# A decode kernel (attention and an MLP, mixed by a gate): sixteen rows of w1 loaded whole to a tile of their own, b1 in three loads

## The chip, the cores and the metric

The kernel runs on one core of one Trainium2 chip. The metric is the device time in microseconds of one execution. Each number given for a kernel is the median of several runs.

## The reference

Eight sequences, one new token each. Attention with 16 query heads over 8 key and value heads of 256, on the last 1,024 positions of a cache; an MLP of 448 to 1,792 to 448 on the layer-normed input; a sigmoid gate that mixes both.

```python
def _A_ref(x, k_cache, v_cache, wq, wo):
    B, Sq, D = x.shape
    Hq, Dh = 16, 256
    Hkv, Sk = k_cache.shape[1], k_cache.shape[2]
    W = min(4096, max(256, Sk // 4))
    rep = Hq // Hkv
    q = (x @ wq).reshape(B, Sq, Hq, Dh).transpose(0, 2, 1, 3)
    k = jnp.repeat(k_cache[:, :, Sk - W:, :], rep, axis=1)
    v = jnp.repeat(v_cache[:, :, Sk - W:, :], rep, axis=1)
    scores = jnp.einsum("bhqd,bhkd->bhqk", q, k) * (Dh ** -0.5)
    p = _softmax(scores, axis=-1)
    o = jnp.einsum("bhqk,bhkd->bhqd", p, v)
    return o.transpose(0, 2, 1, 3).reshape(B, Sq, Hq * Dh) @ wo

def _B_ref(x, w1, b1, w2, b2):
    y = _layernorm(x, axis=-1)
    h = _gelu(jnp.einsum("bsd,df->bsf", y, w1) + b1)
    return jnp.einsum("bsf,fd->bsd", h, w2) + b2

x = A_x
g = _sigmoid((x * gate_w).sum(-1, keepdims=True))
a = _A_ref(x, A_k_cache, A_v_cache, A_wq, A_wo)
b = _B_ref(x, B_w1, B_b1, B_w2, B_b2)
return g * a + (1 - g) * b
```

All tensors are bfloat16. The caches hold 4,096 positions, of which the last 1,024 are read: 33.6 MB of keys and as many of values. wq is 448 x 4,096, wo 4,096 x 448, w1 448 x 1,792, w2 1,792 x 448.

## The kernel before

**Loads.** Nearly all bytes pass through a ring of four slots of 32 KB on each of the 128 partitions (`ring`, `slot`). The list `plan` holds the loads in order: wq; five key quarters (a quarter is the keys of four sequences at a quarter of the positions); then values of one sequence and the next key quarter in turn; the remaining values; w1 (with room for w2 behind it, the slot `w12`); the last sequence's values in two halves, and w2; wo in eight cuts that get smaller. `pump()` issues a load on SP's queue when a slot is free, and `done()` frees one when its last reader has been written down. SP waits for the readers of the slot, and for the completion of an older load where a completion counter is used again (loads take turns on eight counters). The small tensors x and gate_w come on ACT's queue at the start. `biases()`, called after the second key quarter, loads b2 to eight partitions, and b1 as four rows to partitions 0, 32, 64 and 96.

**Order of the work.** The order on each engine is that of the program; it is written out by hand. `query()` projects the queries. For each key quarter `transpose_keys` turns the keys (PE with an evacuation by ACT or DVE; part of each quarter by DVE and POOL), `scores` multiplies. After four quarters a softmax (`top`, `expo`, `turn`) follows, then per sequence `scale`, `bring`, `values`, `finish` and `spread`. `moments()` and `gate()` stand near the start; `norm()` stands after the values of sequence 4, `mlp_hidden()` before the values of the last sequence. The end is `wide` and `narrow`, the matmuls with w2 and wo in the order in which the cuts land, and `run_on` puts matmuls without use between them.

**x, turned.** `turned(a, put, copy)` writes the rows of x (a = 0, for the query) or of the normed x (a = 1, for w1) to a tile `xs`, transposes it on DVE to `xt` and copies it to `xw`, from where PE takes its weights. Rows 0 to 383 of wq and w1 lie three to a partition. The last 64 rows (`DM` to `D`) lie as 128 half rows, one on each partition: half h of row r on partition 2r + h. For these x is written twice, once on the even and once on the odd columns, with the other columns zero (lines 248 and 249), and `ends` makes one matmul for each column quarter pair (line 612).

**w1.** In `mlp_hidden` twelve matmuls (line 601) take the three rows of each partition for four column quarters of 448; the four quarters write to rows 0, 32, 64 and 96 of one PSUM bank. Two more (line 612) add the half rows. Then DVE and ACT compute the GELU and DVE the transposed `hs`.

**Tiles.** `consts` are tiles of their own. `work` tiles share a buffer by tag: w0 holds xs, qs and z in turn, w1 xs and za, w2 xt, qt and zb, w3 xt and zt. `prod` (gate) and `early` (end) lie in `consts`. `shift` is a tile that nothing reads; it moves those behind it, the ring among them.

Of the kernel before, what the change touches and what calls it, by code (L numbers as in the profile page):

```python
# [11 lines left out]
BF16 = mybir.dt.bfloat16  # L12
F32 = mybir.dt.float32
# [4 lines left out]
def kernel(  # L18
# [15 lines left out]
    nc = tc.nc  # L34
    P = nc.NUM_PARTITIONS
# [8 lines left out]
    F = B_w1.shape[1]  # L44
# [31 lines left out]
    TAIL = 12  # L76
    SHIFT = 96
    EARLY = 4
    TURNED = {5: 3, 6: 3, 7: 3}
    FAR = -3.0e38  # L80
# [61 lines left out]
    def rows_loader(pieces):  # L142
        def load(t):
            o = 0
            for ap in pieces:
                n = ap.shape[-1]
                nc.sync.dma_start(t[:, o : o + n], ap)
                o += n

        return load  # L150
# [3 lines left out]
    w1_m = B_w1[0:DM, :].rearrange("(p r) f -> p (r f)", r=NR)  # L154
    w1_t = B_w1[DM:D, :].rearrange("r (h n) -> (r h) n", h=2)
    w2_v = B_w2.rearrange("(p c) n -> p (c n)", c=FB)
# [40 lines left out]
    def biases():  # L197
# [3 lines left out]
        parts = B_b1.rearrange("(t d) -> t d", t=QD)  # L201
        for t in range(QD):
            nc.sync.dma_start(b1_r[BL * t : BL * t + 1, :], parts[t : t + 1, :])

# [9 lines left out]
    xw = consts.tile([P, 2, NX, GAP], BF16)  # L214
    xs = [work.tile([BL, NX, P], BF16, tag=f"w{a}", name="xs") for a in range(2)]
    nc.gpsimd.memset(xs[0][:], 0.0)
# [26 lines left out]
    def turned(a, put, copy):  # L243
        dst = xs[a][0:NB]
        put(
            dst[:, 0:NR, :], x_sb[:, 0:DM].rearrange("b (p r) -> b r p", r=NR)
        )
        for h in range(2):
            put(dst[:, NR + h, h::2], x_sb[:, DM:D])
        xt = work.tile([BL, NX, QD, BL], BF16, tag=f"w{2 + a}", name="xt")  # L250
        nc.vector.transpose(
# [3 lines left out]
        for i in range(QD):  # L255
            copy(xw[BL * i : BL * (i + 1), a, :, BL : BL + NB], xt[:, :, i, 0:NB])  # L256

# [20 lines left out]
    def gate():  # L278
        prod = consts.tile([NB, D], F32)
        gl = consts.tile([NB, 1], F32)  # L280
# [314 lines left out]
    def mlp_hidden():  # L595
        nc.vector.memset(hp, 0.0)
        w = slot("w12")
        for r in range(NR):
            for t in range(QD):
# [7 lines left out]
                    skip_group_check=True,  # L607
                )
        for x2 in range(2):
            lhsT, m = ends(1, x2)  # L610
            o = OW1T + x2 * FQ
            nc.tensor.matmul(
                hp[0:m, :],
                lhsT=lhsT,
                rhs=w[:, o : o + FQ],
                start=False,
# [106 lines left out]
    part = [1, 0, 1, 0, 0, 1, 1, 0, 0, 0, 0, 0, 0]  # L723
    early = consts.tile([2 * BL, DO], F32)
    res = consts.tile([2 * BL, DO], BF16)
# [47 lines left out]
```

## Time and profile before

| what | value |
|---|---|
| median of 3 runs | 189.57 us (189.55 to 190.25) |
| profiled execution | 189.50 us, span 187.6 us, 2,781 instructions |
| PE busy | 126.7 us (68%) |
| DVE, ACT, POOL busy | 94.1 (50%), 72.4 (39%), 80.7 us (43%) |
| bytes moved | 77.85 MB, mean 415 GB/s over the span |
| granted TensorE clock | 0.85 mean |

The profile page gives the span in 40 equal slices, one digit for each, in tenths of busy time:

```
PE   0252498998988987489868985883660167537973
DVE  6602247664654665870653281492045972357711
ACT  2003389691955929740770473274034010001000
POOL 8401591672827538003995999199800000000000
DMA  6999999999999999999999999999999999999991
```

A slice is 4.7 us. Rows of groups, chain and timeline name a line of the kernel (L601), an engine (PE matmul, PEld weight load, DVE, ACT, POOL, SPq for SP's queue of loads), and the tiles, output first. In a timeline row the first number is the start, the second the busy time, and what stands in brackets at the end is the idle time of the engine before it and what ended it. In a row of windows each engine has its busy time and, in parentheses, how many instructions; behind them stand the granted clock, the share of busy time of the 16 DMA engines and the GB/s. The rows of DMA queues have the packets, MB and the share of 16 engines' span.

### The profile page before, as it was taken

What the parts mean: (1) busy time and instruction counts of PE and PEld (TensorE: products, weight loads), DVE (VectorE), ACT (ScalarE), POOL (GpSimd) and SP (SyncE); (2) the same over time, 40 slices, a digit from 0 to 9 for tenths busy, and PEclk for the clock granted to TensorE, in tenths of its full rate; (3) what the DMA queues carried; (4) which work ended last, traced back from release to release, by engine and by line L of the source; (5) the groups of instructions that cost most, each with busy time, mean ns of one, the idle gap of its engine ahead of it and who ended that gap; (6) DMA issues with size and microseconds to landing.
All of it is one profiled execution on the core that took longest, in us unless ns stands there. A gap on an engine that the chain in (4) does not pass through costs nothing.

```text
span 187.6 us, 2781 instructions
## 1 busy us (share of the span) xinstructions
PE 126.7 (68%) x1105; PEld 73.3 (39%) x1106; DVE 94.1 (50%) x161; ACT 72.4 (39%) x87; POOL 80.7 (43%) x157
## 2 busy tenths in 40 slices
PE   0252498998988987489868985883660167537973
PEld 0010485675756655353742671563120012212321
DVE  6602247664654665870653281492045972357711
ACT  2003389691955929740770473274034010001000
POOL 8401591672827538003995999199800000000000
PEclk9999579999999999657997999999576555785798
DMA  6999999999999999999999999999999999999991
GB/s 218 438 465 447 447 412 419 430 414 447 437 447 391 424 470 393 437 423 458 454 398 416 447 426 447 402 440 423 433 433 426 433 423 424 430 423 433 414 400 55
DMA packets 5715, 77.85 MB, mean 415 GB/s; under 512 B 556, under 2 KB 1096, under 8 KB 1864
## 3 DMA queue, kind: packets, MB, share of 16 engines
q1 hardware_dynamic: 5656, 77.68, 97.1%
q8 instruction: 8, 0.13, 0.2%
q10 hardware_dynamic: 48, 0.02, 0.1%
q14 instruction: 3, 0.02, 0.0%
HBM read 77.69 MB, written 0.01 MB: 414 GB/s over the span
## 4 chain that ended last, share of the span: by engine, by line
DMA 27%; PE 25%; POOL 20%; ACT 13%; DVE 11%; issue 3%; SPq 1%; POOLq 0%; ACTq 0%
POOL kt L371 20%; PE ktp L392 14%; DMA slot<-in_A_k_cache_dram 10%; DMA slot<-in_A_wo_dram 9%; ACT kt L396 8%; PE S_ps L467 7%; DMA slot<-in_A_v_cache_dram 7%; PE PO L552 3%; DVE kt L398 2%; ACT E L491 2%; ACT other L491 2%; DVE EB L507 1%; DVE B L357 1%; DVE nmx L480 1%; DVE E L505 1%
## 5 line engine op out<-in xcount | busy, mean ns | idle before, releaser
L371 POOL COPY kt<-B 32x128 f32<-32x128 f32 (+1 forms) x128 | 72.3, 565 | 42.9 <-PE S_ps L467 24.9
L392 PE MATMUL ktp<-ident_f,slot 128*128 128x128 f32 x456 | 64.5, 292 | 14.1 <-DMA slot<-in_A_k_cache_dram 5.9
L396 ACT COPY kt<-ktp 128x1024 bf16<-128x1024 bf16 x57 | 56.3, 1015 | 45.7 <-PE ktp L392 45.7
L392 PEld LDWEIGHTS ktp<-ident_f,slot 128*128 128x128 f32 x456 | 52.4, 148 | 27.8 <-ACT kt L396 11.1
L398 DVE COPY kt<-ktp 128x1024 bf16<-128x1024 bf16 x57 | 38.9, 688 | 31.5 <-PE ktp L392 31.0
L467 PE MATMUL S_ps<-kt,qw 128*16 128x512 bf16 x256 | 21.1, 459 | 12.1 <-POOL kt L371 9.3
L552 PE MATMUL PO<-slot,ET 128*16 128x512 bf16 x256 | 23.3, 523 | 4.8 <-DVE rstd L321 2.0
L357 DVE STREAM_TRANSPOSE B<-slot 128x512 f32<-128x512 f32 (+1 forms) x8 | 8.8, 1105 | 14.4 <-DMA slot<-in_A_k_cache_dram 9.9
L467 PEld LDWEIGHTS <-qw 128*16 128x16 bf16 x256 | 6.6, 92 | 23.8 <-issue 13.4
L552 PEld LDWEIGHTS <-ET 128*16 128x16 bf16 x256 | 7.8, 113 | 18.1 <-issue 11.8
L527 PE MATMUL sm<-EZ,perm 128*128 128x128 bf16 x8 | 2.0, 248 | 13.5 <-DVE EZ L514 13.5
L409 PE MATMUL S_ps<-slot,xw 128*8 128x512 bf16 x24 | 2.9, 617 | 10.7 <-DVE xw L256 7.1
L480 DVE TENSOR_REDUCE nmx<-S_ps 128x1 f32<-128x2048 f32 x2 | 4.6, 2292 | 9.8 <-PE S_ps L467 9.8
L567 DVE STREAM_TRANSPOSE T<-PO 128x512 f32<-128x512 f32 x8 | 5.7, 706 | 7.4 <-PE PO L552 7.4
L629 ACT ACTIVATE zb<-za 128x448 f32<-128x448 f32 x1 | 0.6, 576 | 19.1 <-DVE za L628 19.1
L491 ACT ACTIVATE E<-S_ps,nmx 128x1024 f32<-128x1024 f32 x2 | 4.1, 2036 | 9.7 <-DVE nmx L480 9.7
L527 PEld LDWEIGHTS <-perm 128*128 128x128 bf16 x8 | 0.8, 100 | 16.9 <-DVE EZ L514 16.9
L447 POOL COPY qw<-qt 32x64 bf16<-32x64 bf16 x8 | 2.2, 277 | 11.3 <-DVE qt L434 11.0
L535 DVE TENSOR_TENSOR ET<-sm,mask 128x512 bf16<-128x512 f32 x8 | 5.5, 686 | 1.1 <-PE sm L527 1.0
L434 DVE STREAM_TRANSPOSE qt<-qs 128x512 bf16<-128x512 bf16 x2 | 1.3, 690 | 8.8 <-ACT qs L431 8.8
L702 PE MATMUL warm<-slot,ident 128*128 128x512 bf16 (+1 forms) x17 | 5.4, 421 | 0.2 <-issue 0.2
L409 PEld LDWEIGHTS <-xw 128*8 128x8 bf16 x24 | 0.6, 100 | 12.0 <-POOL b_r L239 7.1
(91 smaller groups left out, 68.9 us busy)
## 6 DMA issues: line engine op xcount, KB each, us to landing
slot<-in_A_k_cache_dram SPq DMA_DIRECT2D x8, 4096.0 KB, 30.2
slot<-in_A_v_cache_dram SPq DMA_DIRECT2D x7, 4096.0 KB, 25.1
slot<-in_A_v_cache_dram SPq DMA_DIRECT2D x2, 2048.0 KB
slot<-in_A_wq_dram SPq DMA_DIRECT2D x1, 2048.0 KB
slot<-in_A_wo_dram SPq DMA_DIRECT2D x2, 896.0 KB
slot<-in_B_w_dram SPq DMA_DIRECT2D x1, 1568.0 KB
slot<-in_B_w_dram SPq DMA_DIRECT2D x1, 1344.0 KB, 22.4
slot<-in_A_wo_dram SPq DMA_DIRECT2D x3, 448.0 KB, 20.6
```

What stands on the lines that cost most here:

```text
L357: nc.vector.transpose(B[:].rearrange("p c w x -> p (c w x)"), kn[:, 0 : n * P],)
L371: nc.gpsimd.tensor_copy(words[BL * w : BL * (w + 1), BL * g : BL * (g + 1), 0:n, 0], B[BL * g : BL * (g + 1), :, w].rearrange("p c x -> p ...
L392: nc.tensor.transpose(words[:, c, :, 0], kn[:, o : o + P], ident_f[:])
L396: nc.scalar.copy(dst, src)
L398: nc.vector.tensor_copy(dst, src)
L467: nc.tensor.matmul(S_ps[BL * t : BL * t + HR, k * QN : (k + 1) * QN], lhsT=qf[:, o : o + HR], rhs=KT[0][:, x : x + n, :, j], start=False, ...
L480: nc.vector.reduce_max(nmx[:], S_ps[:], axis=AXIS.X, negate=True)
L491: nc.scalar.activation((E[:, 0:W], other[:])[u].rearrange("p (c k s) -> p k s c", k=KQ, c=NCK), S_ps[:].rearrange("p (k u s c) -> p u k s ...
L535: nc.vector.tensor_tensor(ET[:].rearrange("p c u a r -> p (c u) a r"), sm[:] .rearrange("p k (o r) -> p k o r", o=1) .to_broadcast([P, NCK ...
L552: nc.tensor.matmul(PO[BL * t : BL * t + Hq], lhsT=ET[:, c].rearrange("p u a r -> p (u a r)"), rhs=vn[:, c], start=(c < QD), stop=(c >= NCK ...
L567: nc.vector.transpose(T[:, 0 : NG * n], PO[:].rearrange("p u (e j) -> p u j e", j=J8))
L702: nc.tensor.matmul(warm[:, 0:m], lhsT=ident[:], rhs=slot("v", NB - 1)[:, 0:m], start=True, stop=True,)
```

## The change

Of w1's last 64 rows 48 are loaded as before, as half rows, now to 96 partitions. The last sixteen are loaded whole, to a tile `w1x` of 16 partitions, in one transfer whose source is four times four rows: row 4j + i goes to partition 4i + j. The transfer is issued after b1 on SP's queue. x gets a sixth block for these rows (a = 1 only), which goes by way of `xt` to the tile `x1x`, and `mlp_hidden` gets four matmuls with it, one for each column quarter. b1 is loaded in three transfers (rows 0 and 1, row 2, row 3). `prod` and `early` move to `work` buffers w0 and w1, and `shift` grows from 96 to 120 columns; with it the ring, and all that lies behind, lies 1,024 bytes further than before on each partition. SP issues as many loads as before.

```diff
-    SHIFT = 96
+    SHIFT = 120
     EARLY = 4
+    NE = 4 * QD
...
-                nc.sync.dma_start(t[:, o : o + n], ap)
+                nc.sync.dma_start(t[0 : ap.shape[0], o : o + n], ap)
...
-    w1_t = B_w1[DM:D, :].rearrange("r (h n) -> (r h) n", h=2)
+    w1_t = B_w1[DM : D - NE, :].rearrange("r (h n) -> (r h) n", h=2)
+    w1_e = B_w1[D - NE : D, :].rearrange("(j i) f -> i j f", i=4)
+    NT = w1_t.shape[0]
...
-        for t in range(QD):
-            nc.sync.dma_start(b1_r[BL * t : BL * t + 1, :], parts[t : t + 1, :])
+        for t, n in ((0, 2), (2, 1), (3, 1)):
+            nc.sync.dma_start(b1_r[BL * t : BL * (t + n) : BL, :], parts[t : t + n, :])
+        nc.sync.dma_start(w1x[:], w1_e)
...
-    xs = [work.tile([BL, NX, P], BF16, tag=f"w{a}", name="xs") for a in range(2)]
+    xs = [
+        work.tile([BL, NX + a, P], BF16, tag=f"w{a}", name="xs") for a in range(2)
+    ]
+    w1x = consts.tile([NE, F], BF16)
+    x1x = consts.tile([BL, NB], BF16)
...
+        n = P - a * (P - NT)
         for h in range(2):
-            put(dst[:, NR + h, h::2], x_sb[:, DM:D])
-        xt = work.tile([BL, NX, QD, BL], BF16, tag=f"w{2 + a}", name="xt")
+            put(dst[:, NR + h, h:n:2], x_sb[:, DM : DM + n // 2])
+        if a:
+            put(
+                dst[:, NX, 0:NE].rearrange("b (i j) -> b i j", i=4),
+                x_sb[:, D - NE : D].rearrange("b (j i) -> b i j", i=4),
+            )
+        xt = work.tile([BL, NX + a, QD, BL], BF16, tag=f"w{2 + a}", name="xt")
...
-            copy(xw[BL * i : BL * (i + 1), a, :, BL : BL + NB], xt[:, :, i, 0:NB])
+            copy(xw[BL * i : BL * (i + 1), a, :, BL : BL + NB], xt[:, 0:NX, i, 0:NB])
+        if a:
+            copy(x1x[:], xt[:, NX, 0, 0:NB])
...
-        prod = consts.tile([NB, D], F32)
+        prod = work.tile([NB, D], F32, tag="w0", name="prod")
...
+        for t in range(QD):
+            nc.tensor.matmul(
+                hp[BL * t : BL * t + NB, :],
+                lhsT=x1x[0:NE, :],
+                rhs=w1x[:, t * FQ : (t + 1) * FQ],
+                start=False,
+                stop=False,
+                skip_group_check=True,
+            )
         for x2 in range(2):
             lhsT, m = ends(1, x2)
             o = OW1T + x2 * FQ
             nc.tensor.matmul(
                 hp[0:m, :],
-                lhsT=lhsT,
-                rhs=w[:, o : o + FQ],
+                lhsT=lhsT[0:NT],
+                rhs=w[0:NT, o : o + FQ],
...
-    early = consts.tile([2 * BL, DO], F32)
+    early = work.tile([2 * BL, DO], F32, tag="w1", name="early")
```

## The prediction, made before the changed kernel ran

> **What bounds the kernel now.** I read the DMA queues on the page first, then the chain of waits, then the last two microseconds by windows, and last the stretches in which the changed instructions stand.
>
> ```profile
> q1 hardware_dynamic: 5656, 77.68, 97.1%
> q8 instruction: 8, 0.13, 0.2%
> q10 hardware_dynamic: 48, 0.02, 0.1%
> q14 instruction: 3, 0.02, 0.0%
> ```
>
> Queue 1, which SP feeds, keeps the 16 DMA engines busy for 97.1% of 187.6 us, 182.2 us: all of the span but the start and the last 3.4 us. The chain of waits ends in it, and after it comes only a short tail:
>
> ```profile
> 153.21 13.89 DMA slot<-in_A_v_cache_dram
> 167.12 16.82 DMA slot<-in_A_wo_dram
> 183.94 0.04 issue
> 183.99 0.92 PE S_ps L730 x12
> 184.93 0.38 DVE res L740
> ```
>
> No load starves it: the shortest lead is that of the key load issued at 82.48, whose predecessor's first engine is done at 88.40. So the time is the stream's, and work on PE, DVE, ACT and POOL is free while it stays inside these leads. The end of the stream is not sharp:
>
> ```profile
> 180.00:182.40 2.40, 1.57 (x18) 0.49 (x18) 0.62 (x1) 0.00 (x0) 0.00 (x0) 1.00 1.03 410
> 182.40:182.80 0.40, 0.40 (x12) 0.28 (x13) 0.00 (x0) 0.00 (x0) 0.00 (x0) 1.00 0.84 323
> 182.80:183.20 0.40, 0.40 (x8) 0.09 (x3) 0.00 (x0) 0.00 (x0) 0.00 (x0) 1.00 0.73 289
> 183.20:183.60 0.40, 0.29 (x3) 0.10 (x1) 0.29 (x1) 0.00 (x0) 0.00 (x0) 1.00 0.57 213
> 183.60:184.00 0.40, 0.01 (x2) 0.01 (x4) 0.11 (x1) 0.00 (x0) 0.00 (x0) 1.00 0.55 186
> 184.00:184.40 0.40, 0.40 (x10) 0.38 (x11) 0.00 (x0) 0.00 (x0) 0.00 (x0) 1.00 0.14 45
> ```
>
> The last two columns are DMA share and GB/s: engines run dry one after another from 182.4 to 184.3. The packet records of the trace (start, length, size, queue; no engine name) show why. Each load of 128 rows ends with 16 four-byte completions, one per engine, and their pattern repeats from load to load, so I can follow 16 lanes. In the last load they finish, in us after the first at 182.44, at 0, 0, 0.01, 0.31, 0.56, 0.64, 0.94, 1.28, 1.52, 1.53, 1.55, 1.62, 1.71, 1.72, 1.77 and 1.81 (184.25). They started within 0.47. What spread them is the instruction fetches: each of the eight 16 KB packets of queue 8 puts one lane back by 1.42 us, each of the three 8 KB packets of queue 14 one lane by 0.5 to 0.8, and no lane gets two. The last matmul's weights load at 184.63, 0.38 after the slowest completion; so one lane, the slowest, sets the end one for one.
>
> Eight lanes carry the rows of x, gate_w and b2 (loads of eight rows), and one of these carries all four rows of b1 as well: after the value load at 69.42 its completions follow each other at 43 ns, five of them. At the end that lane stands at 0.64, and the other seven at 0, 0.01, 0.56, 0.94, 1.28, 1.52 and 1.55.
>
> **The change, part by part.** *Bytes.* w1's last 64 rows were 128 half rows of 1,792 B, eight on each lane. Now 96 stay, six per lane. In the old tail load eight packets and a completion took 0.574 us on the first lane (159.560 to 160.134), 71 ns a packet: every lane saves 2 x 71 = 0.142 us.
>
> The other sixteen rows are packets of 3,584 B. The wo load with that size took 1.097 us for eight and a completion, 136 ns each. On how many lanes they lie no row of before shows directly. Rows bound it: a load of one row used one lane, one of eight rows eight, one of 128 all 16, and the eight include the one. The new load has 16 rows in the tile, and four times four in the source. Between sixteen lanes (0.136 + 0.006 each, which gives back exactly the 0.142) and four lanes (4 x 0.136 + 0.006 = 0.552 each, net +0.410) I take four, among the eight and with b1's lane in them, because the source's outer dimension is four; the other end stays as a rival.
>
> The Trainium skill, "DMA: Bandwidth & Descriptors", section "Why a DMA increments its semaphore by 16 and not by 1", says that the engine count is the largest up to 16 that divides the slowest dimension of both sides and that the lowest-numbered engines are used; the trace agrees for one and eight rows, and no run here shows a four. The same page's section "Rules for kernel authors" speaks against the change: a small outer dimension confines a transfer to that many engines, so use a multiple of 16. By that rule the load costs each of its engines 0.55 us and not 0.14, and the sum becomes that of the first rival below.
>
> *b1.* Three loads, of two, one and one row: b1's lane has 43 ns less, another of the four 43 ns more.
>
> *The sum.* The slowest lane, if not among the four, ends 0.142 earlier: 1.81 - 0.14 = 1.66. A lane among the four is moved to its place plus 0.41: b1's to 1.01, 0.56 to 0.97, 0.94 to 1.35 or 1.40, 1.28 to 1.69 or 1.73, 1.52 to 1.93 or 1.98, 1.55 to 1.96 or 2.00. So the sum depends on which three lanes join b1's. With neither 1.52 nor 1.55 the end comes 0.14 earlier (0.08 to 0.12 with 1.28 among them); with either, 0.13 to 0.20 later. Of the 35 ways to choose three of seven, 10 are of the first kind. Two readings weigh against that count. In the first load the lane at 0 starts first (1.739) and the one at 0.56 next (1.763), before most others of the eight (1.52 at 1.765, 1.28 at 1.782) and before the eight that carry no small rows (1.785 to 2.083), as if engines were started in rising order. And the large fetches hit six of those eight higher lanes, but only two of the lower eight, so more probably at their upper end. I take the early three: -0.142 us.
>
> *Everything else is covered.* SP issues as many loads as before (a b1 issue took 0.23 to 0.25 us; a 128-row wo issue 0.33), and its next issue after them stood 8.8 us later. w1x flows near 70 us, and is read near 168.6. On POOL the memset of xs grows from 640 to 768 columns, 0.62 to some 0.74, and the b1_r memset behind it by as much; PE's first matmul waits for that, but then stands 3.55 us for wq. In the norm:
>
> ```profile
> 149.61 1.11 DVE L324 TENSOR_SCALAR xs<-x_sb,mv,rstd 8x384 bf16<-8x384 bf16 x3
> 150.76 0.83 DVE L251 STREAM_TRANSPOSE xt<-xs 32x640 bf16<-32x640 bf16 x1
> 151.63 0.92 ACT L256 COPY xw<-xt 32x40 bf16<-32x40 bf16 x4 [8.69 <-DVE xt L251]
> 153.22 0.72 DVE L567 STREAM_TRANSPOSE T<-PO 128x512 f32<-128x512 f32 x1 [0.72 <-PE PO L552]
> ...
> 168.57 0.61 PE L612 MATMUL S_ps<-slot,xw 128*72 128x448 bf16 x2
> ...
> 172.23 1.89 PE L552 MATMUL PO<-slot,ET 128*16 128x512 bf16 x16 [1.23 <-DMA slot<-in_A_v_cache_dram]
> ```
>
> DVE gets one more pass of 0.30 (the short ones of L324 take 303 to 307 ns) and a transpose 768/640 as long, +0.17: 0.47 inside the 0.72 that it stands idle before L567. ACT gets one copy of 0.22, needed 14 us later. PE gets four matmuls with their weights: twelve of L601 took 0.74, so 0.25, or 0.63 if another pause of 0.38 comes as before L612. The hidden layer's chain shifts by that; on PE it vanishes in the 1.23 before 172.23, and on DVE it moves the end of oP from 177.16 to 177.8 at most, before the matmuls that read it at 178.11. Without these covers it would cost 0.25 to 0.63. prod and early move to buffers whose last readers were done long before (za at 173.3, early at 183.31).
>
> The profiled execution took 189.50, its span 187.6 and 1.9 around it; the median of the three runs is 189.57. From the median: 189.57 - 0.14 = 189.43.
>
> **The rivals.** *A late lane among the four.* The place is the lane at 1.52 or 1.55; it decides as soon as a lane later than 1.40 is among the four (1.40 + 0.41 = 1.81). For it: the count of 25 in 35, and that 1.52 starts only 2 ns after 0.56. Against: the two readings above. Time: 189.57 + 0.13 to 0.20, 189.70 to 189.77, a little slower than before.
>
> *An extra instruction fetch.* PE gets eight instructions, DVE and ACT one each. For 2,211 on PE there were eight 16 KB packets, so eight more are unlikely to ask for a ninth; if one comes, or one is moved onto a lane that has had one, that lane is 1.4 back. On the slowest: 1.81 - 0.14 + 1.42 = 3.09, which is 1.28 later, 190.85; on a middle lane (1.28 - 0.14 + 1.42 = 2.56), 0.75 later, 190.3. It decides from a lane at 0.53 on. Against: the code before 168 us is unchanged on PE, and the fetch times hang on it.
>
> *Sixteen lanes after all*, so that the change doesn't move bytes: 0.142 taken and given, 189.5 to 189.6.
>
> A gain of more than 0.5% has hardly a place: the mean of the 16 lanes ends at 1.06, so even a perfect balance of the same bytes brings 0.74 us.
>
> **How the numbers follow.** Forecast 0.50; late lane 0.30; sixteen lanes 0.06; extra fetch 0.09; something not seen in the tail or a lead 0.05. 0.5% of 189.57 is 0.95 us, about what a measurement of this kernel can tell from no change (the three runs lie 0.70 apart). Forecast, late lane and sixteen lanes are all within it, the middle-lane half of an extra fetch too, but I leave weight for costs that I don't see: same 0.83, slower 0.12, faster 0.05. The range runs from 0.2 under the forecast to the middle-lane fetch's lower part, 189.25 to 190.1.
>
> **What would show it.** Sixteen packets of 3,584 B near 70 us: four in a row on each of four lanes, with four completions, or one on each of sixteen. Then the last completions: the latest at 184.11 and all ends closer together, or one of the eight lanes alone behind the rest by 0.1 to 0.3. Queue 8 with 8 packets and queue 14 with 3, or more. DVE still idle before T at 153.2, and PE still waiting for the value load at 172. A lead on SP that shrinks to nothing, or a tail after the last completion longer than 3.4 us, would make the prediction wrong in its kind.

## The result and the profile after

The changed kernel takes 190.33 us (189.89 to 193.47, 22 runs) and the kernel before, measured beside it, 189.61 (189.47 to 190.33, 22 runs): ratio 1.0035, 95% interval 1.0022 to 1.0048. The run of 193.47 us is a slow one, over 1.5% above the fastest, and is left out of the ratio and of the means below. The change makes the kernel slower by 0.35%. That lies inside the 0.5% which the prediction called no change, but above its range, and the sign is the other one: 0.72 us longer by the medians in place of 0.14 shorter.

The chain of waits of the changed kernel, its last five steps (start, us, engine, tiles), ends as it did before:

```profile
153.16 14.51 DMA slot<-in_A_v_cache_dram
167.69 16.73 DMA slot<-in_A_wo_dram
184.41 0.04 issue
184.46 0.84 PE S_ps L755 x12
185.32 0.38 DVE res L765
```

The stream of loads still sets the end, and the last matmuls follow it as before; they start at 184.46, where they started at 183.99. So the stream itself ends later, though it moves the same 77.68 MB in fewer packets (page, DMA queues):

```profile
q1 hardware_dynamic: 5644, 77.68, 97.2%
q8 instruction: 8, 0.13, 0.2%
...
q14 instruction: 3, 0.02, 0.0%
```

The end by windows (columns as in the prediction, DMA share and GB/s last):

```profile
180.00:182.40 2.40, 1.96 (x16) 0.55 (x14) 0.34 (x1) 0.00 (x0) 0.00 (x0) 1.00 1.02 410
182.40:182.80 0.40, 0.06 (x4) 0.06 (x8) 0.28 (x1) 0.00 (x0) 0.00 (x0) 1.00 1.07 408
182.80:183.20 0.40, 0.40 (x12) 0.23 (x13) 0.00 (x0) 0.00 (x0) 0.00 (x0) 1.00 0.92 363
183.20:183.60 0.40, 0.40 (x8) 0.09 (x3) 0.00 (x0) 0.00 (x0) 0.00 (x0) 1.00 0.78 311
183.60:184.00 0.40, 0.34 (x5) 0.10 (x1) 0.24 (x1) 0.00 (x0) 0.00 (x0) 1.00 0.66 235
184.00:184.40 0.40, 0.00 (x0) 0.00 (x0) 0.16 (x1) 0.00 (x0) 0.00 (x0) 1.00 0.58 195
184.40:184.80 0.40, 0.34 (x8) 0.33 (x10) 0.00 (x0) 0.00 (x0) 0.00 (x0) 1.00 0.08 27
```

The run-out has the shape of before, moved by one row: 363, 311, 235, 195, 27 GB/s where before had 323, 289, 213, 186, 45 one row earlier. Not one lane is late but all of them. Where they lost it is seen in the windows around w1's tail, where nothing was expected but a saving. First before, then after:

```profile
161.00:162.00 1.00, 0.34 (x8) 0.21 (x12) 0.61 (x1) 0.00 (x0) 0.00 (x0) 1.00 1.11 455
162.00:163.00 1.00, 1.00 (x20) 0.35 (x12) 0.00 (x0) 0.00 (x0) 0.00 (x0) 0.57 1.00 426
```

```profile
161.00:162.00 1.00, 0.55 (x12) 0.31 (x16) 0.39 (x1) 0.00 (x0) 0.00 (x0) 1.00 1.04 331
162.00:163.00 1.00, 1.00 (x28) 0.40 (x16) 0.00 (x0) 0.00 (x0) 0.00 (x0) 1.00 0.98 374
```

The DMA engines are as busy as before (1.04 and 0.98) but move 331 and 374 GB/s in place of 455 and 426. In the packet records the packets themselves are longer there: 8,192 B packets, which take 309 ns elsewhere, take up to 509, and the tail's half rows, 74 ns in before, up to 124. It happens to all lanes alike: from the load ahead of the tail to the load behind it, the 16 completions of after keep their places to each other within 0.04 us.

To put numbers on it I use the completions again. Their mean over the 16 lanes, from one load to another, leaves out how the lanes are scattered: a *b1 step* (from the fifth key load to the sixth; b2, b1 and the new load lie between) and a *tail step* (from the last value load ahead of w1 to the first half of the last sequence's values; w1 with its tail lies between). *Lengthening* is what the packets that start from 160 to 163 us took beyond the usual time of their size, summed over all lanes. Span and what lies outside it (time less span) are means over the runs, in us; the steps and the lengthening are those of the one profiled run of each kernel. The row of before takes in its runs beside all the experiments:

```
kernel       runs   span  outside  b1 step  tail step  lengthening
before        133 187.73    1.96    19.608     8.677        0
after          21 188.13    2.28    19.810     8.913       6.2
e1_shift       12 187.61    1.96    19.655     8.676        0
e2_tail96      12 188.08    1.96    19.623     8.924       6.5
e3_tail128     11 187.75    2.21    19.819     8.677        0
e4_sixteen      6 188.58    2.18    20.134     9.229      11.1
e5_halves       6 188.58    1.90    19.609     9.388      11.4
e6_evens       11 187.67    1.92    19.608     8.682        0
e7_far          6 188.45    1.97    20.442     8.676        0
e8_again        8 188.06    2.18    19.830     8.979       7.3
e9_spread      11 187.80    2.36    19.610     8.679        0
e10_pe         12 187.73    2.19
e11_dve        12 187.71    2.02
e12_act        12 187.65    1.98
e13_both       12 188.24    2.03    19.644     9.276      10.0
e14_counts     11 188.13    1.99    19.762     8.963       7.1
e15_joined     12 187.89    2.17    19.612     8.679        0
e16_pairs       1 187.9     1.9     19.769     8.826       5.0
e17_ones        1 189.5     1.9     19.609     8.919       3.9
e18_order       1 187.9     2.1     19.722     8.824       2.6
```

The first two rows divide the loss: the span grows by 0.40 (interval some 0.28 to 0.52), what lies outside it by 0.32 (0.12 to 0.52). So there are two losses, and only one of them is in the span. The tail step tells kernels apart well: 8.676 to 8.682 wherever nothing is lengthened, and 8.913, 8.979 and 8.963 in the three profiles with the changed tail load (after, e8, e14). The b1 step scatters more: e16 and e18 load no rows of w1 near 70 us, and still have 0.16 and 0.11 more than before.

### The profile page after: what moved, and what is told of

Read it like the earlier page. It is cut to its first block, busy times and chain, and to the rows that moved or that the text cites. A ratio compares the mean times of both kernels' runs of the same rounds, so it can differ in the third digit from the quotient of the medians.

```text
span 188.0 us, 2792 instructions
## 1 busy us (share of the span) xinstructions
PE 127.2 (68%) x1110; PEld 73.7 (39%) x1110; DVE 94.5 (50%) x162; ACT 72.5 (39%) x88; POOL 81.2 (43%) x157
## 3 DMA queue, kind: packets, MB, share of 16 engines
q1 hardware_dynamic: 5644, 77.68, 97.2%
## 4 chain that ended last, share of the span: by engine, by line
DMA 39%; PE 26%; ACT 14%; DVE 11%; POOL 5%; issue 2%; SPq 1%; POOLq 0%; ACTq 0%; DVEq 0%
DMA slot<-in_A_k_cache_dram 22%; PE ktp L408 15%; ACT kt L412 9%; DMA slot<-in_A_wo_dram 9%; DMA slot<-in_A_v_cache_dram 8%; PE S_ps L483 7%; POOL kt L387 5%; PE PO L568 3%; DVE kt L414 3%; ACT E L507 2%; ACT other L507 2%; DVE EB L523 1%; DVE B L373 1%; DVE nmx L496 1%; DVE E L521 1%
## 5 line engine op out<-in xcount | busy, mean ns | idle before, releaser
L568 PE MATMUL PO<-slot,ET 128*16 128x512 bf16 x256 | 22.0, 501 | 5.3 <-DVE rstd L337 2.0
L727 PE MATMUL warm<-slot,ident 128*128 128x512 bf16 (+1 forms) x18 | 5.9, 447 | 0.0
```

The costliest lines, as they stand in the source:

```text
L568: nc.tensor.matmul(PO[BL * t : BL * t + Hq], lhsT=ET[:, c].rearrange("p u a r -> p (u a r)"), rhs=vn[:, c], start=(c < QD), stop=(c >= NCK ...
L727: nc.tensor.matmul(warm[:, 0:m], lhsT=ident[:], rhs=slot("v", NB - 1)[:, 0:m], start=True, stop=True,)
```

## The experiments

### The address, and each half of the change alone

The change moves the ring by 1,024 bytes, shortens the tail load, and adds a load. The first three kernels take these apart. *e1_shift* is the kernel before with the ring moved:

```diff
-    SHIFT = 96
+    SHIFT = 352
```

> The kernel before with shift at 352 columns, so that the ring and all behind it lies 1,024 bytes further, as in the changed kernel; nothing else. Theory 1 (the tail load on 96 partitions slows all lanes) and theory 2 (the four-lane load and its contention): no effect, 189.6 us, no packet longer than its size's usual length except beside instruction fetches. Theory 3 (the new addresses make the small lengthenings between 37 and 61 us, some 0.75 us summed over the lanes, and the wider scatter of the times): 189.9 to 190.3, those lengthenings in the trace, scatter as in the changed kernel.

Measured: 189.55, ratio 0.9995 (0.9986 to 1.0004), the tail step as before, the b1 step 0.05 longer. The address doesn't show in the time. Its slowest completion, though, stood at 184.424 in the profile against 184.249 before, with the same loads: a single profile places the end only to some 0.2 us, and so the readings here rest on the mean steps of the lanes and on the spans of several runs.

*e2_tail96* is the kernel before with the shorter tail load, and nothing in place of the sixteen rows:

```diff
-    w1_t = B_w1[DM:D, :].rearrange("r (h n) -> (r h) n", h=2)
+    w1_t = B_w1[DM : D - 16, :].rearrange("r (h n) -> (r h) n", h=2)
...
-                lhsT=lhsT,
-                rhs=w[:, o : o + FQ],
+                lhsT=lhsT[0:96],
+                rhs=w[0:96, o : o + FQ],
```

> The kernel before, with the tail of w1 loaded as 96 half rows to 96 partitions; the last sixteen rows of w1 are left out of load and matmul, so 57 KB less is moved. Theory 1: the packets around that load (160 to 163 us) are lengthened by some 6 us summed over 16 lanes, 0.39 us a lane, against 0.14 saved: the slowest completion about 0.24 later, 189.85. Theories 2 and 3, and the prediction's sum: none lengthened, 0.14 saved, 189.45.

*e3_tail128* is the other half, the changed kernel that loads all 128 half rows besides:

```diff
-    w1_t = B_w1[DM : D - NE, :].rearrange("r (h n) -> (r h) n", h=2)
+    w1_t = B_w1[DM:D, :].rearrange("r (h n) -> (r h) n", h=2)
...
-    NT = w1_t.shape[0]
+    NT = P - 2 * NE
```

> The changed kernel, with all 64 tail rows loaded as 128 half rows again (the last 32 half rows are loaded and not used); w1x stays. Theory 1: no lengthened packets at 160 to 163 us, eight packets a lane instead of six (+0.14), 0.39 regained, so 0.24 less than the changed kernel, 190.1. Theory 2: 0.14 more than the changed kernel, 190.5.

Measured: e2 189.92, ratio 1.0023 (1.0010 to 1.0036); e3 189.81, ratio 1.0013 (1.0001 to 1.0025). Loading a quarter less of the tail makes the kernel slower by itself. e2's tail step is 8.924 where 8.677 - 0.142 = 8.535 was due, 0.39 too long on the mean of the lanes, and its 161 to 162 window shows it without the added load:

```profile
161.00:162.00 1.00, 0.69 (x16) 0.35 (x20) 0.26 (x1) 0.00 (x0) 0.00 (x0) 1.00 1.01 308
162.00:163.00 1.00, 1.00 (x20) 0.42 (x16) 0.00 (x0) 0.00 (x0) 0.00 (x0) 0.79 0.98 393
```

e3 is the opposite: its span is that of before (187.75), although four of its lanes carry 0.55 us more. So none of the four is the last lane, which the prediction could not decide. Its loss is all outside the span (2.21). The two losses, 0.23% and 0.13%, add up to the 0.35% of the change.

### Sixteen lanes in place of four

*e4_sixteen* loads the sixteen rows in their natural order, one to a partition and a lane:

```diff
-    w1_e = B_w1[D - NE : D, :].rearrange("(j i) f -> i j f", i=4)
+    w1_e = B_w1[D - NE : D, :]
...
-                dst[:, NX, 0:NE].rearrange("b (i j) -> b i j", i=4),
-                x_sb[:, D - NE : D].rearrange("b (j i) -> b i j", i=4),
+                dst[:, NX, 0:NE],
+                x_sb[:, D - NE : D],
```

> The changed kernel, with w1x loaded in the order of its rows, sixteen by one, so that each of 16 lanes gets one packet of 3,584 bytes. Theory 1: the slowest lane of the changed kernel was none of the four, so it gets 0.14 more, 190.3 to 190.5; the lengthened packets at 160 to 163 us stay. Theory 2: the four lanes lose 0.41 and no contention at 70 us, 190.0 to 190.1.

Measured: 190.70, ratio 1.0057 (1.0044 to 1.0070). The bytes on a lane are the same on the mean (0.138 or 0.142 us), but the b1 step is 20.134, 0.53 longer than before; in after it is 0.20 longer. The Trainium skill, "DMA: Bandwidth & Descriptors", section "Rules for kernel authors", advises an outermost dimension that is a multiple of 16; here sixteen lanes that write to sixteen neighbouring partitions cost 0.32 more on the mean of the lanes than four lanes do with the same rows, so the measurement goes against it for this load. The tail step is longer than in after too (9.229), with the same tail load, so the load alone doesn't set its cost; how the lanes stand to each other when they reach it may be the rest, which no run here shows by itself.

### Which partitions a load covers

Theory: a load that is not dealt over the partitions like one of 128 rows lengthens all packets in flight. *e5_halves* and *e6_evens* are the kernel before with the same 128 half rows at the same places, in two loads of 64: the lower and the upper half, or the even and the odd partitions:

```diff
-                nc.sync.dma_start(t[:, o : o + n], ap)
+                if o == OW1T:
+                    for k in range(2):
+                        nc.sync.dma_start(
+                            t[P // 2 * k : P // 2 * (k + 1), o : o + n],
+                            ap[P // 2 * k : P // 2 * (k + 1)],
+                        )
+                else:
+                    nc.sync.dma_start(t[:, o : o + n], ap)
```

```diff
-                nc.sync.dma_start(t[:, o : o + n], ap)
+                if o == OW1T:
+                    for k in range(2):
+                        nc.sync.dma_start(t[k::2, o : o + n], ap[k::2])
+                else:
+                    nc.sync.dma_start(t[:, o : o + n], ap)
```

> The kernel before, with the tail of w1 (128 half rows, all 128 partitions as before) loaded by two transfers of 64 partitions each, 0 to 63 and 64 to 127. The same packets on each lane, four and four. Theory A (an engine may write only the partitions that it writes in a 128-row load without holding up others; a transfer of fewer rows deals them out otherwise): packets around 161 us lengthened, the mean step from the last full value load to the next 0.2 to 0.5 us longer than the 8.677 of before, time 189.8 to 190.1. Theory B (it is the shorter and uneven transfer itself, 96 rows, that costs): 8.68 and 189.6, one completion more.

> As the run with two halves, but one transfer takes the even and the other the odd partitions, so that each engine's four rows spread over eight neighbouring partitions. Theory A: the rows fall on all partitions evenly, so less than in the run with two halves: a step of 8.7 to 8.9, 189.6 to 189.8. Theory B: as with two halves, 8.68. If any load of other than 128 rows costs the same wherever it goes, the same step as the run with two halves.

Measured: e5 190.48, ratio 1.0049 (1.0036 to 1.0061); e6 189.56, ratio 0.9998 (0.9989 to 1.0006). The same windows, e5 first:

```profile
161.00:162.00 1.00, 1.00 (x12) 0.29 (x8) 0.00 (x0) 0.00 (x0) 0.00 (x0) 0.50 0.90 273
162.00:163.00 1.00, 1.00 (x16) 0.35 (x12) 0.00 (x0) 0.00 (x0) 0.00 (x0) 0.50 0.97 312
```

```profile
161.00:162.00 1.00, 0.42 (x8) 0.21 (x12) 0.52 (x1) 0.00 (x0) 0.00 (x0) 1.00 1.01 412
162.00:163.00 1.00, 1.00 (x24) 0.50 (x20) 0.00 (x0) 0.00 (x0) 0.00 (x0) 1.00 1.04 442
```

Both issue the same two loads of 64 packets of 1,792 B, with the same bytes on every lane. Half the partitions in one block: 273 GB/s, 0.71 us on every lane. Every second partition: nothing. So it is neither the bytes, nor the number of loads, nor their size. (With the partitions, the rows that one load reads from DRAM differ between the two as well; e7 below keeps them.) The Trainium skill, "DMA: Bandwidth & Descriptors", section "Rules for kernel authors", says of two transfers to disjoint partition halves that one transfer over all 128 should be used instead, since they share the same engines anyway; the trace agrees with the advice, at a price of 0.71 us that the section does not give.

*e7_far* is e3 with the sixteen rows at partitions 64 to 79 in place of 0 to 15:

```diff
+    FAR0 = 64
...
-        nc.sync.dma_start(w1x[:], w1_e)
+        nc.sync.dma_start(w1x[FAR0 : FAR0 + NE], w1_e)
...
```

> The run with w1's tail on 128 partitions (w1x by four lanes), but w1x lies on partitions 64 to 79 and not 0 to 15. Theory A: the four lanes write there what other engines write in 128-row loads, so the step from the last early key load to the next, 19.82 with w1x at 0 to 15, becomes 19.87 to 19.97, and lengthened packets at 69 to 71 us are more than the 0.7 us of that run. Theory B: 19.82 and 0.7, 189.8.

Measured: 190.43, ratio 1.0041 (1.0028 to 1.0053), b1 step 20.442. The window of 70 to 71 us, in after and in e7:

```profile
70.00:71.00 1.00, 0.64 (x6) 0.42 (x4) 1.00 (x1) 1.00 (x2) 0.92 (x3) 1.00 1.22 515
```

```profile
70.00:71.00 1.00, 0.65 (x4) 0.42 (x4) 1.00 (x2) 1.00 (x3) 0.92 (x3) 1.00 0.80 247
```

247 GB/s in place of 515. (Packets of 32 KB take 1.2 us there, so a window of 1 us is coarse; over the three from 69 to 72 us it is 394 in place of 504.) Against e3 only the place of the partitions differs: the same rows are read, in the same order and in packets of the same size. So for this load it is the partitions written that decide, and not the reading from DRAM: 0.62 us on the mean of the lanes between 0 to 15 and 64 to 79 (20.442 and 19.819).

*e8_again* is the changed kernel once more, beside these.

> The changed kernel once more, unchanged, for its times and its lanes beside those of the other runs. All theories: 190.0 to 190.4; the steps 19.81 and 8.91 again, whichever lanes the fetches hit.

Measured: 190.28, ratio 1.0030 (1.0017 to 1.0043), tail step 8.979, lengthening 7.3. The loss comes again, at the same place.

### A tail load that should cost nothing

If 64 half rows at every second partition are harmless, 96 half rows can be loaded so: *e9_spread* is the changed kernel with 64 of them on every second and 32 on every fourth partition, and the sixteen rows behind them in place of beside b1:

```diff
-                nc.sync.dma_start(t[0 : ap.shape[0], o : o + n], ap)
+                if o == OW1T:
+                    nc.sync.dma_start(tail[0::2, :], ap[0 : P // 2])
+                    nc.sync.dma_start(tail[1::4, :], ap[P // 2 :])
+                    nc.sync.dma_start(t[0:NE, OW1X : OW1X + F], w1_e)
+                else:
+                    nc.sync.dma_start(t[:, o : o + n], ap)
...
-            put(dst[:, NR + h, h:n:2], x_sb[:, DM : DM + n // 2])
+            if a:
+                put(dst[:, NR + h, 2 * h :: 4], x_sb[:, DM : DM + BL])
+                put(dst[:, NR + h, 1 + 4 * h :: 8], x_sb[:, DM + BL : D - NE])
...
```

> The change with its loads laid out by theory A: the 96 half rows of the tail go to a tile of their own, set to zero once, 64 of them to the even partitions and 32 to every fourth from 1 on (two loads), so that the rows fall evenly on all partitions; w1x goes to partitions 0 to 15 of the w1 slot, by four lanes as in the change, right behind the tail. Theory A: hardly a lengthened packet at 160 to 163 us but for w1x's own (0.7 to 1.0 us), the lanes outside the four 0.14 earlier than before and the four 0.41 later; if none of the four is the last, 189.4 to 189.6, beside 190.3 for the change. Theory B (uneven or shorter loads cost): as the change, 190.1 to 190.3.

Measured: no lengthening, and a tail step of 8.679 that now has the sixteen rows in it: 8.677 - 0.142 + 0.138 = 8.673 by bytes alone. The slowest completion of its profile stands at 184.138, 0.11 before that of the kernel before, as the prediction's sum had it (though within the 0.2 of a single profile). And yet the time is 189.96, ratio 1.0024 (1.0010 to 1.0039): the span's mean is 187.80, what lies outside it 2.36, the most of all kernels. The first loss is gone here; the second is not.

### What lies outside the span

The packet records show what goes with the second loss: an instruction fetch after the last matmul. In after an 8 KB packet of queue 14 starts at 189.805, behind the end of the span (so that the page's row still counts three); e9 has one of 8 KB at 189.239 and one of 16 KB at 190.267; before, e2, e5 and e6 have none there. Of the twenty profiled runs ten have such a packet. In nine of these 1.98 to 3.38 us lie outside the span, and the packet, or the later of two, starts 1.8 to 2.7 us after its end; in e10's it starts 1.05 us after it, and 1.88 lie outside. Of the ten without, nine have 1.88 to 1.91 outside, and e13's 2.19. One of those with it is e1's (8 KB at 189.958, 2.53 outside), whose instructions are those of before; so more instructions can make such a fetch more frequent, but it comes without them too. Which engine's instructions bring it? Three kernels add to the kernel before what the change adds to one engine: four matmuls with their weights on PE, one instruction on DVE, one on ACT.

```diff
+    run_on(4, 16)
```

```diff
+        nc.vector.memset(accs[:, 0:8], 0.0)
```

```diff
+        nc.scalar.copy(stats[:, 0:1], mv[:, 0:1])
```

> The kernel before with four small matmuls more on PE (eight instructions, as many as the change adds) behind the first seven fill matmuls; nothing reads them. What lies outside the span was 1.92 us in the median for the kernel before and for the runs with its instruction counts, and 2.09 to 2.23 for the changed kernel and most runs with its counts, whose traces have one or two instruction fetches more, after the span. Theory P (PE's eight instructions bring the late fetch): 2.1 outside, 189.8. Theory D or A (the one more on DVE or on ACT does): 1.92 and 189.6.

> The kernel before with one more instruction on DVE, a memset of 8 columns in the norm (accs, written again later). Theory D: 2.1 us outside the span, a late fetch of 8 KB in the trace, 189.8. Theories P and A: 1.92, 189.6.

> The kernel before with one more instruction on ACT, a copy of 8 values in the norm that nothing reads. Theory A: 2.1 us outside the span, a late fetch of 8 KB in the trace, 189.8. Theories P and D: 1.92, 189.6. If all three stay at 1.92, only the sum of them, or something else of the change, brings it.

Measured: ratios 1.0010 (0.9993 to 1.0027), 1.0000 (0.9988 to 1.0011), 0.9990 (0.9979 to 1.0001). By time none differs from before for certain. By the records two do: e10 has a 16 KB fetch at 188.741, e11 one of 8 KB at 189.338, e12 none. And the part outside the span is above 2.0 in 10% of the runs of before, in 50% of e10's, 58% of e11's, 8% of e12's (twelve runs each), and 81% of the changed kernel's. So the instructions added on PE and on DVE each make a late fetch more frequent, and for the one on ACT the runs show nothing of it.

*e14_counts* is the changed kernel, meant to have no more instructions on PE and DVE than before: one memset moved to POOL, and three long matmuls without use in place of seven short ones.

```diff
-    nc.vector.memset(eps_t[:], 1e-5)
+    nc.gpsimd.memset(eps_t[:], 1e-5)
...
-    run_on(FILL[0])
+    for _ in range(3):
+        nc.tensor.matmul(
+            warm[:], lhsT=ident_f[:], rhs=E[:, 0:QN], start=True, stop=True
+        )
```

> The changed kernel, loads as they are, but with no more instructions on PE and DVE than the kernel before: three long fp32 fill matmuls for the first seven, one memset moved from DVE to POOL. If the late fetches come from these counts: no fetch after the span, 1.92 us outside it and not 2.09, span 188.0 to 188.1, 190.0. If not: 2.1 outside and 190.2.

Measured: 189.90, ratio 1.0024 (1.0005 to 1.0044); no late fetch in the profile, 1.99 outside the span, and the span's 188.13 of the changed kernel. So most of the second loss is taken away here, and the first is left. Beside the changed kernel's 2.28, what lies outside is 0.29 us less on the mean and 0.16 in the median (1.93 in place of 2.09): six of the 21 runs of the changed kernel have 2.3 or more and draw its mean up.

Only DVE's count is back, though. The profiles of before, after, e14 and, from further below, e15 count:

```profile
PE 126.7 (68%) x1105; PEld 73.3 (39%) x1106; DVE 94.1 (50%) x161; ACT 72.4 (39%) x87; POOL 80.7 (43%) x157
PE 127.2 (68%) x1110; PEld 73.7 (39%) x1110; DVE 94.5 (50%) x162; ACT 72.5 (39%) x88; POOL 81.2 (43%) x157
PE 125.5 (67%) x1108; PEld 72.4 (39%) x1109; DVE 95.4 (51%) x161; ACT 72.4 (39%) x88; POOL 80.9 (43%) x158
PE 128.7 (69%) x1109; PEld 73.8 (39%) x1109; DVE 94.4 (50%) x161; ACT 72.6 (39%) x88; POOL 81.8 (44%) x159
```

The three fp32 matmuls of the program stand in the trace of e14 as six matmuls with six weight loads, so by these rows PE still has six instructions more than before in e14 and seven in e15 (nine in after by the same count, where the program adds eight; a record or two can be missing). What e14 shows is therefore the return of DVE's one instruction; no run has the loads of the changed kernel and PE's count of before.

The Trainium skill, "Runtime: NRT & Kernel Launch", section "Instruction fetch mechanics", says that an engine fetches its code in blocks of 16 KiB, 256 instructions, ahead of need, and that crossing into the next is mostly hidden. The traces have packets of 16 KB and also of 8 KB. Inside the span each sets one lane back (1.42 us, or 0.5 to 0.8) and costs nothing when that lane isn't the last; one that starts late after the span goes with the longer times above.

### Both losses at once, and what the place alone does not explain

*e13_both* was to join the two: counts as before (PE's are not: 1,109 matmuls and 1,110 weight loads in its profile), and the 48 rows whole, on partitions that follow e9's pattern.

```diff
+        nc.sync.dma_start(tail[0::4, :], w1_t[:, 0::2])
+        nc.sync.dma_start(tail[2::8, :], w1_t[:, 1])
+        nc.sync.dma_start(t[0:NE, OW1X : OW1X + F], w1_e)
```

> The idea of the change without the two costs found. The 48 rows of the tail lie whole on partitions 8g, 8g + 2 and 8g + 4 of a tile set to zero (two loads, spread evenly), w1x on partitions 0 to 15 by four lanes; PE and DVE have no more instructions than in the kernel before (fewer fill matmuls, the long ones in fp32; one write of x for the tail and not two). If tail and late fetches are the whole loss: no lengthened packets, the step 8.68 or less, 1.92 us outside the span, 189.5 to 189.65, at or a little under the kernel before. If something else of the change costs as well: 189.8 or more.

Measured: 190.21, ratio 1.0031 (1.0020 to 1.0043). Outside the span 2.03, near before; but the tail step is 9.276 and the lengthening 10.0, as bad as e5. My reading until then, that a load is harmless if each lane writes only its own eight neighbouring partitions, fits e5, e6 and e9 and falls here. *e16_pairs* keeps only the first of the two loads, *e17_ones* only the second, and *e18_order* both, with the rows in natural order so that neither skips any in DRAM.

> e13_both without its load of sixteen whole rows to partitions 2::8 (these rows of w1 are left out of the result): 32 whole rows on partitions 0::4 remain, two packets of 3,584 B on each lane, and the sixteen rows behind them. If whole rows, or this load, lengthen the packets in flight: some 5 to 10 us of lengthening summed over the lanes at 160 to 162 us. If the other load does it: none, and the step from v6 to v7a is 8.68 - 0.14 * 1 = 8.5 on the mean plus 0.13 for the sixteen rows.

> e13_both without its load of 32 whole rows to partitions 0::4 (these rows of w1 are left out of the result): sixteen whole rows on partitions 2::8 remain, one packet on each lane, and the sixteen rows behind them. If whole rows, or this load, lengthen the packets in flight: some 3 to 10 us of lengthening at 160 to 162 us. If the other load does it: none. If neither e16_pairs nor e17_ones shows it, it takes both together.

> e13_both with the 48 whole rows in their natural order: rows 0 to 31 of them to partitions 0::4, rows 32 to 47 to partitions 2::8, so that each load reads one contiguous piece of DRAM as those of e9_spread do, while packet size (3,584 B), partitions and counts stay as in e13_both. If the source that skips rows lengthened the packets: step from v6 to v7a 8.67 to 8.70, no lengthening at 160 to 162 us. If whole rows on these partitions did: 9.2 to 9.3, some 10 us of lengthening summed over the lanes, as in e13_both.

Measured, one run each: 189.77, 191.35 and 189.99 us; lengthening 5.0 in e16, 3.9 in e17 up to 163 us, 2.6 in e18. Either load does it alone, so it doesn't take both together. As far as single runs can tell, the order in DRAM has a part: without skipped rows three quarters of the lengthening of e13 are gone, but not all of it. And e17 goes on. Its windows at 170 and 175 us, and those of before, where the loads are the same:

```profile
170.00:175.00 5.00, 2.53 (x25) 0.66 (x17) 3.39 (x8) 0.58 (x1) 0.00 (x0) 0.50 1.03 395
175.00:180.00 5.00, 5.00 (x21) 1.78 (x22) 2.36 (x6) 0.00 (x0) 0.00 (x0) 0.70 0.99 376
```

```profile
170.00:175.00 5.00, 3.55 (x30) 1.03 (x24) 4.19 (x8) 0.58 (x1) 0.00 (x0) 0.50 1.00 420
175.00:180.00 5.00, 4.85 (x35) 1.51 (x35) 1.98 (x6) 0.00 (x0) 0.00 (x0) 0.92 1.00 415
```

395 and 376 GB/s in the first pair, 420 and 415 in the second, 10 us and more after the odd load was done. Until the stream ends nine in ten of e17's packets of 3,584 B and more are longer, most of 8,192 B by about a tenth (342 to 345 ns in place of 309), and the run took 191.35, with less to load than any other. It begins with the odd load, so it reads as if such a load could leave the lanes so that they hinder each other afterwards; one run doesn't show that it was this and nothing from outside the kernel. What the lanes share is open for these loads: e7 against e3 points to the partitions written, e18 against e13 to the rows read.

*e15_joined* takes the loads of e9, which show no lengthening, and the counts of e14, with e9's two pairs of passes in the norm made one pass each:

```diff
-                put(dst[:, NR + h, 2 * h :: 4], x_sb[:, DM : DM + BL])
-                put(dst[:, NR + h, 1 + 4 * h :: 8], x_sb[:, DM + BL : D - NE])
...
+            flat = dst.rearrange("b r c -> b (r c)")
+            for n, o, s, k in ((BL, 0, 4, DM), (NE, 1, 8, DM + BL)):
+                wide_h = P + s // 2
+                put(
+                    flat[:, NR * P : NR * P + 2 * wide_h].rearrange(
+                        "b (h c) -> b h c", h=2
+                    )[:, :, o : o + s * (n - 1) + 1 : s],
+                    x_sb[:, k : k + n]
+                    .rearrange("b (o r) -> b o r", o=1)
+                    .to_broadcast([NB, 2, n]),
+                )
```

> The loads of e9_spread (96 half rows as 64 on every second partition and 32 on every fourth, the last sixteen rows behind them) with the instruction counts brought back: four passes in the norm instead of six, the memset of eps_t on POOL, and three fp32 matmuls of 128x512 without use in place of the first seven of run_on. Theory (both causes found: partitions of the tail load, and a fetch after the end): slowest completion 184.1 to 184.2 as in e9_spread, nothing fetched after the span, 1.92 outside the span, so 189.45 to 189.55, 0.05 to 0.15 under the kernel before. Rival (the spread loads themselves cost time outside the span): 189.9 as e9_spread.

Measured: 189.90, ratio 1.0020 (1.0003 to 1.0037). The steps are e9's, without lengthening, but the span's mean is 187.89 (187.72 to 188.06), not below before, and half of the runs have more than 2.0 outside the span. The profiled run has no late fetch and 1.88 outside; the expected 189.45 to 189.55 did not come. Why half of the runs are long is open: PE's count is still above that of before (the rows above), as in e10, where half of the runs are long too, and the kernel has more instructions than e14 on POOL and on SP; none of these was taken back alone. No version that I ran beats the kernel before.

## Why the prediction was wrong

**What bounds the kernel, and the lane that ends last:** right. The chain ends in the stream again, the slowest completion moves from 184.249 to 184.682 and the matmuls behind it by 0.47.

**"Every lane saves 2 x 71 = 0.142 us":** this is the step that failed. It priced the 96 half rows by the 71 ns that a packet took in a load of 128. The 71 ns did not hold for the changed load: after's tail step is 8.913 in place of 8.535, 0.38 us more on every lane, and e2, with this edit alone, shows the same (0.39). The row from which I took the 71 ns was that of a load over all 128 partitions, and nothing in the trace of before showed one over 96; so it was an operation not shown, and its cost should have been bounded from both sides. I had bounded the lanes and not the rate.

**Four lanes, among the eight and with b1's:** right. The sixteen packets of 3,584 B form four chains between 69.31 and 70.62 us, four in a row each, mostly 136 ns apart. The Trainium skill's rule on how many engines a load uses ("DMA: Bandwidth & Descriptors", "Why a DMA increments its semaphore by 16 and not by 1") gave four, and the trace agrees. The b1 step is 0.20 us longer on the mean of the lanes where the load's bytes make 0.138; there are lengthened packets in after between 69 and 71 us, but 0.06 is no more than this step scatters without the load (e16, e18).

**The early three:** right in what it was for. The four lanes end 0.74, 1.24, 1.41 and 1.44 us after the first, the last lane of all 1.83. The late lane, the rival with the largest chance, did not happen, and e3's unchanged span (187.75) says the same over eleven runs. That it was the early lanes the runs show; that it was for the two slight readings on which the choice rested, they do not.

**"Eight more are unlikely to ask for a ninth":** the second failed step. In after's profile it is not PE's ninth of 16 KB but one of 8 KB after the end; e10 shows that PE's does come, and e11 that one instruction on DVE is enough. I looked for its price on a lane of the stream (0.75 or 1.28) and did not see that it may come when the stream is over, where it touches no lane: what lies outside the span is 0.29 us longer on the mean in after than in e14, which has DVE's count of before.

**The sum, as it came out:** -0.14 for the tail's bytes, +0.38 for its lengthening, +0.06 at the added load, and the added bytes on lanes that are not last; 0.30 together, while the span grew by 0.40 (0.28 to 0.52). With 0.32 outside the span that is 0.62 of the 0.72.

**The covers:** they held. In after's norm the fourth pass and the longer transpose end just ahead of the transpose of PO, which starts at 153.17 (before 153.22) and has next to no idle time before it (timeline):

```profile
149.88 1.29 DVE L340 TENSOR_SCALAR xs<-x_sb,mv,rstd 8x384 bf16<-8x384 bf16 x4
151.21 0.97 DVE L265 STREAM_TRANSPOSE xt<-xs 32x768 bf16<-32x768 bf16 x1
...
152.65 0.43 DVE L351 TENSOR_SCALAR b2s<-b_b,om 8x448 f32<-8x448 bf16 x1
...
153.16 0.20 ACT L272 COPY x1x<-xt 32x8 bf16<-32x8 bf16 x1
...
153.17 0.72 DVE L583 STREAM_TRANSPOSE T<-PO 128x512 f32<-128x512 f32 x1
```

Of the 0.72 that DVE stood idle there 0.09 are left (153.08, where L351 ends, to 153.17). The pass and the transpose took 0.18 and 0.14 of them, a little less than forecast (0.30 and 0.17), and the norm began 0.27 later, with the stream. On PE the four matmuls took 0.54, between the 0.25 and 0.63 of the forecast, and PE still waits for the value load afterwards, longer than before (1.69, before 1.23), since the load is later:

```profile
167.64 0.54 PE L626 MATMUL S_ps<-w1x,x1x 16*8 16x448 bf16 x4
...
168.11 0.96 PE L637 MATMUL S_ps<-slot,xw 96*72 96x448 bf16 x2
...
172.57 1.03 PE L568 MATMUL PO<-slot,ET 128*16 128x512 bf16 x8 [1.69 <-DMA slot<-in_A_v_cache_dram]
```

**The range:** 189.25 to 190.1 took in the late lane and the lower part of a fetch in the stream, and no cost of the tail load itself. It should have left the rate of a 96-row load open upwards. How far, no row of before says: a tenth of the step that the load stands in (8.68 us) would have taken the range to 189.43 + 0.87 = 190.30, but that tenth is chosen afterwards.

## What to carry to other kernels

Where the stream of loads sets the time, a load's price is not its bytes: look at the GB/s of the window around it beside the DMA share, since a share of 1.0 with fewer GB/s went here with lengthened packets. Leave loads over all 128 partitions whole, and if a part must be loaded, spread it (every second partition cost nothing here, half of them in a block 0.71 us a lane) and measure it alone, because the pattern that is harmless was not to be had from a rule. And an instruction on an idle engine need not be free for being covered: count what the change adds to each engine, and look at what lies between the span's end and the time.

## What was not expected of the hardware

- Two loads of 64 packets each, with the same bytes on every lane, differ by 0.71 us on each lane by the partitions that they cover and the rows that go there (e5, e6); the same sixteen rows on four lanes cost 0.62 more on the mean of the lanes at partitions 64 to 79 than at 0 to 15 (e7, e3).
- After one odd load of sixteen packets the stream stayed at 376 to 395 GB/s in place of 415 to 420, until its end 20 us later (e17, one run).
- An instruction fetch after the last matmul shows in no row of the page. Nine of the ten profiled runs with one have 1.98 to 3.38 us outside the span, nine of the ten without 1.88 to 1.91. One added DVE instruction (e11) or eight on PE (e10) made runs with over 2.0 outside five to six times as frequent as in before.
